# An MLP gate row built in four column tiles and spread over the partitions by DMA, and a ScalarE normalisation cut into single instructions

## The chip, the core and the metric

One of the eight cores of a Trainium2 chip runs the whole program. The metric is device time in microseconds (us) for one execution, as the median of several executions; lower is better. The engines are named as the profile names them: PE (TensorE, matrix products), PEld (its weight loads), DVE (VectorE), ACT (ScalarE), POOL (GpSimd) and SP (SyncE, which here only starts transfers). Transfers started by SP run in hardware queue q1, those started by POOL in software queue q0; sixteen DMA engines serve both.

## The reference, cut to what matters

Sequence length S = 2048, model width D = 576, hidden width 4608, bf16 data.

```python
mod = (silu(c) @ w_mod).reshape(1, 6, 1, 576)
sa, ca, ga, sb, cb, gb = (mod[:, k] for k in range(6))
h = layernorm(x) * (1 + ca) + sa
x = x + ga * A(h)          # dilated local attention: 32 heads of 18, 8 keys, every second row
h = layernorm(x) * (1 + cb) + sb
x = x + gb * (((h @ w_gate) * (h @ w_up)) @ w_down)
```

The change concerns gb, the gate row of the MLP: 576 numbers, the same for every row of the sequence, each a dot product of silu(c) with a column of the last sixth of w_mod. It also concerns how one layernorm is written out.

## The kernel before, in words

The 2048 rows are cut into 8 chunks of 256 rows. The chunks are handled in five groups, [0], [1, 2], [3, 4], [5, 6], [7]. For each group the MLP has a gate-up phase (`gate_up`) and a down phase (`down`, `down_last` for the last). In gate-up, step f (0 to 35) makes 128 of the 4608 hidden columns: two products g and u over 576 = 4 x 128 + 64 inputs. They are done as a `Pair`: the array is used as two halves of 64 rows, one for g and one for u; `first()` does the 64-row rest and four half blocks, `second()` swaps the halves. The order on PE is first of step f, then second of step f-1. ACT then copies u and g out of PSUM (lines 757 and 758 for one-chunk groups), and DVE multiplies them (line 760) once per two steps. Weight blocks of four steps (`wgu`, gate half and up half, 512 KB each) come by SP in queue q1; the down weights (`wd`, 576 KB a block) come by POOL in queue q0. PSUM is one pool of 8 banks which are given out in turn (line 91), so a product needs the bank that was given out eight tiles before to have been read.

Into the steps are woven the attention pieces of later chunks. Their order is not found at run time: the function `timed` (lines 808 to 845) walks through the 36 steps with a clock t for PE and one for DVE, and puts a piece behind the first step at which its condition holds. A piece is (PE time, DVE time, marks it needs, its own mark, delay until that mark holds, function). The products of the next chunk (`qkv_of`, nine `Pair`s: four pairs of q and k column tiles, tile 4 on its own, and two for v) are put between steps in the same way, at most one per step. Every engine then executes its instructions in the order in which they were written. SP and POOL too: a transfer that waits for something holds up the transfers behind it on the same engine.

All the changed pieces lie in the gate-up phase of group 0 (some 48 to 98 us in the profile). Named from the trace and the planner:

- Line 1271, the first thread of group 0: `load_wm5` (lines 1015 to 1017: the last sixth of w_mod, 512 rows into the spare part of `hh`, 64 rows into `wm5r`, which the trace calls o_t), `load_wd(0)`, `both_halves`, and, when 12.0 on the planner's clock have passed, `gb_row` at a planned PE time of 1.5.
- `gb_row` (line 1257) calls `mod_row` (lines 349 to 359) and then `ld_d1(3)`, the load of down block 3. `mod_row` has silu(c) on all 128 weight columns (`sc_bc`), so each of its ten products (five with 512 columns into pa, five with 64 into pb) writes the same row on all 128 partitions; two ACT copies bring it to `gb_bc` (f32). `gb_row` stands behind step 11, that is, directly ahead of step 12, which is the first to need weight block 3.
- Weight block 3 lies in the spare part of `hh` too and is loaded at line 1320; block 4 is asked for at step 4, block 5 at step 8, block 6 at step 12.
- `norm_of(3, ...)` (line 683): layernorm of chunk 3: statistics (`a_ln(3)`), `rsq`, two ACT pieces e3 and n3 (one per 128 rows j; each of them `norm_act`, line 283: a small DVE product `ln_nb`, an ACT instruction of 576 columns and one of 64 columns, which doubles the last 64 columns), then `a_td(3)`: two DMA transposes by SP (line 394) into hT, and `a_mod(3)`: five DVE instructions on hT (line 302, planned 8.0 behind the transposes), which set mark h3. The nine pairs of chunk 3 need h3.
- Line 1273: layernorm of chunk 4: `a_ln(4)` on DVE, `rsq`, and two ACT pieces (`norm_act` with 576 columns only, no doubling); in the trace ACT line 287 at 79.00 and 82.65.
- `values_of(1)`: DVE products and sums of the attention of chunk 1 (lines 514, 521 to 524).
- `gb_bc` is read by DVE behind the down products (lines 949, 954 and 996).

Of the kernel before, what the change touches and what calls it, by code (L numbers as in the profile page):

```python
# [7 lines left out]
BF = mybir.dt.bfloat16  # L8
F32 = mybir.dt.float32
ALU = mybir.AluOpType  # L10
# [8 lines left out]
P = 128  # L19
D = 576  # L20
DP = 640
KT = 5
KF = 4
H = 32
# [2 lines left out]
DIL = 2  # L27
FF = 4608
FT = FF // P
HALO = 16  # L30
SPAN = 14
EPS = 1e-5
# [2 lines left out]
ST = CH // P  # L35
# [9 lines left out]
def kernel(  # L45
# [13 lines left out]
    nc = tc.nc  # L59
# [9 lines left out]
    consts = pool("consts", 1)  # L69
    wts = pool("wts", 1)  # L70
    dramp = pool("dramp", 1, space=DRAM)
    xin = pool("xin", 2)
    xres = pool("xres", 2)
    small = pool("small", 2)
# [16 lines left out]
    def ps(shape, dt, name):  # L91
        return psp.tile(shape, dt, name=name, tag="bank")
# [8 lines left out]
    eps = consts.tile([P, 1], F32, name="eps")  # L101
    modc = consts.tile([P, 4, KT], F32, name="modc")
    ga_bc = consts.tile([P, D], F32, name="ga_bc")
    gb_bc = consts.tile([P, D], F32, name="gb_bc")
    sc_bc = consts.tile([P, KT, P], BF, name="sc_bc")
    xns = [consts.tile([P, ST, DP], BF, name=f"xn{k}") for k in range(2)]
    o_sb = consts.tile([P, ST, DP], BF, name="o_sb")
# [5 lines left out]
    wv = wts.tile([P, KT, D], BF, name="wv")  # L113
    wo = wts.tile([P, KT, D], BF, name="wo")
    vd = dramp.tile([HALO + S, D], BF, name="vd")
    prod_t = consts.tile([P, 4 * KT * CH], BF, name="prod_t")
    prod_n = [0]

# [19 lines left out]
    def load_res(i):  # L138
        x_res[i] = xres.tile([P, ST, D], BF, name="x_r")
        nc.sync.dma_start(x_res[i][:], x_rows(i))  # L140

    wgu_blk, wgu_in, wd_blk, wd_home, wgu_home = {}, {}, {}, {}, {}
    NG = len(GROUPS)
    NBLK = FT // FB

# [17 lines left out]
    def load_wd(g):  # L163
        if g >= NG * NBLK:
            return
        r0 = (g % NBLK) * FB * P
        wb = wd_home.pop(g, None)
        if wb is None:
            wb = wdp.tile([P, FB, D], BF, name="wd")
        wd_blk[g] = wb  # L170
        return nc.gpsimd.dma_start(wb[:], B_w_down[r0:r0 + FB * P, :].rearrange("(k p) n -> p k n", p=P))  # L171
# [88 lines left out]
    def ln_parts(src, tag, act=False, both=None):  # L260
        stats = small.tile([P, ST, 2, 6], F32, name="ln_stats" + tag)
        mv = small.tile([P, ST, 2], F32, name="ln_mv" + tag)
        rstd = small.tile([P, ST], F32, name="ln_rstd" + tag)
        xn = xns[turn[0] % 2]
        turn[0] += 1
        both = tag == "b" if both is None else both

        def stat(j, hfs=(0, 1)):
            for hf in hfs:
                nc.vector.bn_stats(stats[:, j, hf, :], src(j)[:, hf * 288:(hf + 1) * 288])  # L270
            if hfs[-1] == 1:
                nc.vector.bn_aggr(mv[:, j, :], stats[:, j, :, :].rearrange("p a b -> p (a b)"))

        def rsq(r):
            nc.scalar.activation(rstd[:, r], mv[:, r, 1], ACTF.Ln, bias=eps[:])
            nc.scalar.activation(rstd[:, r], rstd[:, r], ACTF.Exp, scale=-0.5)

        def norm(j):
            for d0, s0, n in ((0, 0, D), (D, D - 64, 64))[0:2 if both else 1]:
                nc.vector.tensor_scalar(xn[:, j, d0:d0 + n], src(j)[:, s0:s0 + n], mv[:, j, 0:1], rstd[:, j:j + 1],  # L280
                                        ALU.subtract, ALU.mult)

        def norm_act(j):
            nb = small.tile([P, 1], F32, name="ln_nb")
            nc.vector.scalar_tensor_tensor(nb[:], mv[:, j, 0:1], -1.0, rstd[:, j:j + 1], ALU.mult, ALU.mult)
            for d0, s0, n in ((0, 0, D), (D, D - 64, 64))[0:2 if both else 1]:
                nc.scalar.activation(xn[:, j, d0:d0 + n], src(j)[:, s0:s0 + n], ACTF.Identity, bias=nb[:], scale=rstd[:, j:j + 1])
        return xn, stat, rsq, (norm, norm_act) if act is None else norm if not act else norm_act

    def layernorm(src, tag, act=False, both=None):  # L290
        xn, stat, rsq, norm = ln_parts(src, tag, act, both)
        for j in range(ST):
            stat(j)

        def norms(js=range(ST)):
            for j in js:
                norm(j)
        return xn, lambda: rsq(slice(0, ST)), norms

    def modulate(dst, s, m, vi_scale, vi_shift, on_dve):  # L300
# [20 lines left out]
    def mod_columns(wm, pi, fill=lambda: None, steps={}):  # L321
        pm = ps([P, 320], F32, "pm")
        order = (KF, 0, 1, 2, 3)
        for kt in order:
            for q in range(4):
                rows = slice(0, P) if kt < KF else slice(64 * (q // 2), 64 * (q // 2) + 64)
                c0 = (q // 2) * D + (q % 2) * 256
                nc.tensor.matmul(pm[H * q:H * (q + 1), :], lhsT=sc_bc[rows, kt, 0:H], rhs=wm[rows, kt, c0:c0 + 320],
                                 start=(kt == order[0]), stop=(kt == order[-1]), skip_group_check=True)
            steps.get(kt, nop)()  # L330
        mrow = sp.tile([P, 320], BF, name="mrow")
        nc.scalar.copy(mrow[:], pm[:])
        fill()
        tr = ps([P, 3, P], BF, "pm_t")
        for n in range(2):
            nc.tensor.transpose(tr[:, n, :], mrow[:, n * P:(n + 1) * P], ident[:])
        for r in (slice(0, 64), slice(64, P)):
            nc.tensor.transpose(tr[r, 2, :], mrow[:, 2 * P:], ident[:])
        c01 = slice(2 * pi, 2 * pi + 2)

        def adds():
            nc.vector.tensor_tensor(modc[:, c01, 0:KF].rearrange("p b (u v) -> p b u v", v=2),
                                    tr[:, 0:2, :].rearrange("p v (b u x) -> p b u v x", b=2, u=2)[:, :, :, :, 0],
                                    addc[:, :, 0:KF].rearrange("p b (u v) -> p b u v", v=2), ALU.add)
            nc.vector.tensor_tensor(modc[:, c01, KF:KT], tr[:, 2, :].rearrange("p (b x) -> p b x", b=2)[:, :, H:H + 1],
                                    addc[:, :, KF:KT], ALU.add)
        return adds

    def mod_row(wm, dst):
        pa = ps([P, 512], F32, "pa")  # L350
        pb = ps([P, 64], F32, "pb")
        for p_t, c0, c1 in ((pa, 0, 512), (pb, 512, D)):
            for kt in range(KT):
                m = wm(kt)
                rows = slice(0, m.shape[0])
                nc.tensor.matmul(p_t[:], lhsT=sc_bc[rows, kt, :], rhs=m[:, c0:c1],
                                 start=(kt == 0), stop=(kt == KT - 1))
        nc.scalar.copy(dst[:, 0:512], pa[:])
        nc.scalar.copy(dst[:, 512:D], pb[:])
# [3 lines left out]
    aa, bb, h2T, x1 = {}, {}, {}, {}  # L363
# [319 lines left out]
    def norm_of(n, after, free, load=None):  # L683
        def go():
            a_td(n)
            if load is not None:
                load_x(load)
        act = n == 3
        norm = [(0, 0, f"r{n}", f"e{n}", 2.0, lambda: aa[n]["norm"]((0,))), (0, 0, f"e{n}", f"n{n}", 1.6, lambda: aa[n]["norm"]((1,)))]
        if not act:  # L690
            norm = [(0, 1.5, f"r{n}", f"n{n}", 0.3, lambda: aa[n]["norm"]())]
        return [(0, 2.5 if act else 2.3, after, f"m{n}", 0.2, lambda: a_ln(n)), (0, 0, f"m{n}", f"r{n}", 1.0, lambda: aa[n]["rsq"]()),
                *norm, (0, 0, f"n{n} {free}", f"x{n}", 8.0, go),
                (0, 1.6, f"x{n}", f"h{n}", 1.2, lambda: a_mod(n, (4, 0, 1, 2, 3)))]
# [166 lines left out]
    def gate_items(gi):  # L861
        n = len(GROUPS[gi])
        own = 0.15 * n + 0.06
        if gi != 1:
            return [("f", f, 1.0 * n, own, "") for f in range(FT)]
        return [("f0", f, 1.04, 0.28, "") for f in range(HEAD)] + [("f1", f, 1.04, 0.28, "h2") for f in range(HEAD)] + [("f", f, 2.0, own, "") for f in range(HEAD, FT)]

# [43 lines left out]
    def down(gi, hh, bg):  # L911
        grp = GROUPS[gi]
        nj = ST * len(grp)
        last = FT - FB
        at, late = among(last, 0.25 * nj, bg)
# [94 lines left out]
    wm5r = outp.tile([P, D], BF, name="o_t")  # L1010

    def wm5():
        return spare[0][:, 8 * NB:8 * NB + FB * D].rearrange("p (k d) -> p k d", d=D)

    def load_wm5():
        nc.gpsimd.dma_start(wm5(), w_mod[0:KF * P, 5 * D:6 * D].rearrange("(k p) n -> p k n", p=P))
        nc.gpsimd.dma_start(wm5r[0:64, :], w_mod[KF * P:D, 5 * D:6 * D])

# [236 lines left out]
        load_wd(k)  # L1255

    def gb_row():
        mod_row(lambda k: wm5()[:, k, :] if k < KF else wm5r[0:64, :], gb_bc)
        ld_d1(3)

    first = attention_of(1, 2)[12:-14]
# [6 lines left out]
    at = [k for k, p in enumerate(first) if p[3] == "o11"][0] + 2  # L1268
    first[at] = (0.6, 0, "o11", "-", 0, lambda: b_o(1))
    gbg = {0: (qkv_of(3, "p17 z3"),  # L1270
               [[(0, 0, "", "-", 0, lambda: (load_wm5(), load_wd(0))), (0, 0, "", "z3", 8.0, both_halves), (0, 0, "", "w5", 12.0, nop), (1.5, 0, "w5", "-", 0, gb_row), (0, 0, "", "-", 0, lambda: load_res(2))],
                first,
                norm_of(3, "", "", 5) + [(0, 2.5, "", "m4", 0.2, lambda: a_ln(4)), (0, 0, "m4", "r4", 1.0, lambda: aa[4]["rsq"]()),
                                         (0, 0, "r4", "e4", 2.0, lambda: aa[4]["norm"]((0,))), (0, 0, "e4", "n4", 1.6, lambda: aa[4]["norm"]((1,))),
# [37 lines left out]
    for gi, grp in enumerate(GROUPS):  # L1312
        hh_t = hhp.tile([P, FT * 2 * CH], BF, name="hh")
        n = CH * len(grp)
# [45 lines left out]
```

## Time and profile before

| | |
|---|---|
| median of 3 runs | 543.81 us (543.6, 543.81, 544.0) |
| the profiled execution, its own time | 544.44 us |
| its span, first to last instruction | 542.7 us |
| granted PE clock | 1.000 |
| gate row: its ACT copies (lines 358, 359) | 0.585 + 0.218 us |
| ACT line 287, 576 columns; 64 columns | 0.87 us; 0.42 us |
| POOL memset of 64 x 576 bf16 (lines 230, 231, 249) | 0.57 to 0.59 us |
| POOL transfer of 72 KB (line 1017), issue | 0.56 us |
| up half of weight block 3 (SP, issued 41.67), to landing | 22.9 us |
| landing of: w_mod rows, wm5r, wd block 0, wd block 3 | 60.7, 61.0, 63.2, 65.3 us |

The span is shorter than the profiled execution's own time by 1.7 us, which lies outside its instructions. Times inside the trace are counted from the start of the span. Busy shares say little here: a PE matrix product is counted from its start to its end although the next one starts 0.1 us later, so PE is shown busy in many places where it loses up to 0.2 us.

### The profile page before, as it was taken

To read this page: it belongs to the slowest core of one execution; us is meant where nothing else is said; L and a number is where in the kernel's file an instruction comes from. 1 tells how busy PE (TensorE), PEld (TensorE's weight loads), DVE (VectorE), ACT (ScalarE), POOL (GpSimd) and SP (SyncE) were. 2 spreads that over 40 slices of the span, in tenths; PEclk is the share of its full clock that TensorE was granted. 3 is DMA by queue.
4 is the path that set the end of the run, shared out by engine and by line. 5 is a ranking of instruction groups with operands and counts; after the bars stand their busy time and mean duration, and the time that the engine had idled before them with its cause. 6 is when DMAs were issued, how large, how long until landed. Compare 5 with 4: busy or idle time off the path is not lost.

```text
span 542.7 us, 14569 instructions
## 1 busy us (share of the span) xinstructions
PE 535.3 (99%) x6157; PEld 321.9 (59%) x6189; DVE 315.9 (58%) x713; ACT 251.5 (46%) x617; POOL 67.9 (13%) x104
## 2 busy tenths in 40 slices
PE   8999999999999999999999999999999999999997
PEld 4887789756745444555544444555544445558875
DVE  4989586777766777646358896524344924032212
ACT  4776777543566553022645552014555551006630
POOL 7104012122000110111000110110010101010210
PEclk9999999999999999999999999999999999999999
DMA  8999999778872694878435983894296592849821
GB/s 264 299 261 363 336 272 332 258 224 258 267 203 89 211 208 153 227 220 293 135 108 163 232 288 68 162 239 159 89 275 176 156 311 69 255 138 294 271 74 42
DMA packets 94924, 114.52 MB, mean 211 GB/s; under 512 B 27980, under 2 KB 83676, under 8 KB 94732
## 3 DMA queue, kind: packets, MB, share of 16 engines
q1 hardware_dynamic: 83360, 67.29, 44.6%
q0 software_dynamic: 11344, 46.25, 27.8%
q8 instruction: 48, 0.79, 0.6%
q14 instruction: 16, 0.13, 0.1%
q10 hardware_dynamic: 156, 0.07, 0.0%
HBM read 103.15 MB, written 4.74 MB: 199 GB/s over the span
## 4 chain that ended last, share of the span: by engine, by line
PE 94%; DMA 3%; DVE 1%; SPq 1%; ACT 1%; issue 0%
PE pg L706 28%; PE pu L706 23%; PE acc L921 19%; PE pq L706 3%; PE accr L926 3%; PE pw L605 3%; PE pq L416 3%; PE acc L976 3%; PE lgT L470 2%; DMA wmC<-in_w_mod_dram 2%; PE pv L706 2%; PE pv L439 1%; DMA wqk<-in_A_wqkv_dram 1%; PE po L567 1%; PE pwj L584 0%
## 5 line engine op out<-in xcount | busy, mean ns | idle before, releaser
L706 PE MATMUL pg<-h2T,wgu 64*128 64x512 bf16 (+1 forms) x1376 | 265.5, 331 | 0.0
L706 PE MATMUL pu<-h2T,wgu 64*128 64x512 bf16 (+1 forms) x1376 | 264.5, 331 | 0.0
L706 PEld LDWEIGHTS <-wgu 64*128 64x128 bf16 x2752 | 136.5, 94 | 94.8 <-issue 0.5
L757 ACT CAST u_sb<-pu 128x512 bf16<-128x512 f32 (+1 forms) x172 | 85.4, 497 | 135.8 <-PE pg L706 131.2
L760 DVE TENSOR_TENSOR hh<-g_sb,u_sb 128x512 bf16<-128x512 bf16 x136 | 57.4, 423 | 116.2 <-ACT g_sb L758 115.7
L758 ACT CAST g_sb<-pg 128x512 bf16<-128x512 f32 (+1 forms) x172 | 86.7, 504 | 0.0
L921 PEld LDWEIGHTS <-hh 128*128 128x128 bf16 x504 | 49.0, 98 | 59.5 <-issue 1.5
L921 PE MATMUL acc<-wd,hh 128*128 128x512 bf16 x329 | 84.1, 380 | 0.1
L926 PE MATMUL accr<-wd,hh 128*128 128x64 bf16 x344 | 62.4, 193 | 0.7
L706 PE MATMUL pu<-h2T,wgr 64*128 64x512 bf16 (+1 forms) x188 | 61.5, 327 | 0.2 <-ACT u_sb L757 0.2
L706 PE MATMUL pg<-h2T,wgr 64*128 64x512 bf16 (+1 forms) x188 | 61.5, 327 | 0.0
L926 PEld LDWEIGHTS <-hh 128*128 128x128 bf16 x504 | 45.8, 98 | 1.9
L171 POOL DMA_DIRECT2D wd<-in_B_w_down_dram x29 | 21.8, 752 | 190.0 <-PE accr L926 93.4
L461 DVE TENSOR_TENSOR prod_t<-qT,kT 128x1280 bf16<-128x1280 bf16 x56 | 43.7, 818 | 0.7 <-ACT kT L777 0.7
L514 DVE TENSOR_TENSOR vsh<-vsh,attn 128x1152 bf16<-128x1152 bf16 x56 | 39.6, 748 | 1.2 <-DMA vsh<-vd 1.2
L706 PEld LDWEIGHTS <-wgr 64*128 64x128 bf16 x376 | 19.7, 94 | 15.4 <-issue 2.5
L921 PE MATMUL acc<-prod_t,hh 128*128 128x512 bf16 x111 | 28.8, 380 | 0.0
L304 ACT ACTIVATE h2T<-h2T,modc 128x256 bf16<-128x256 bf16 x12 | 6.6, 595 | 45.3 <-DMA h2T<-xn 45.3
L455 POOL DMA_DIRECT2D vsh<-vd x14 | 12.5, 897 | 104.8 <-DVE o_sb L524 89.6
L706 PE MATMUL pq<-hT,wqk 64*128 64x256 bf16 (+1 forms) x360 | 22.2, 259 | 0.1
L416 PE MATMUL pq<-hT,wqk 128*128 128x256 bf16 (+1 forms) x225 | 21.2, 251 | 0.4 <-ACT hT L304 0.4
L926 PE MATMUL accr<-prod_t,hh 128*128 128x64 bf16 x112 | 21.6, 193 | 0.1
(208 smaller groups left out, 605.0 us busy)
## 6 DMA issues: line engine op xcount, KB each, us to landing
wgu<-in_B_w_gate_dram SPq DMA_DIRECT2D x41, 512.0 KB, 4.5
wgu<-in_B_w_up_dram SPq DMA_DIRECT2D x41, 512.0 KB, 6.4
wd<-in_B_w_down_dram POOLq DMA_DIRECT2D x29, 576.0 KB, 5.6
vsh<-vd POOLq DMA_DIRECT2D x14, 1152.0 KB, 9.3
prod_t<-in_B_w_down_dram POOLq DMA_DIRECT2D x8, 576.0 KB, 7.6
hh<-in_B_w_down_dram POOLq DMA_DIRECT2D x6, 576.0 KB, 6.4
x_r<-in_A_x_dram SPq DMA_DIRECT2D x8, 288.0 KB, 8.3
vd<-v_sb POOLq DMA_DIRECT2D x16, 144.0 KB, 5.2
```

Source lines behind the costliest of these rows:

```text
L171: return nc.gpsimd.dma_start(wb[:], B_w_down[r0:r0 + FB * P, :].rearrange("(k p) n -> p k n", p=P))
L416: nc.tensor.matmul(pq[:, gi, :], lhsT=wqk[:, kt, m * P:(m + 1) * P], rhs=hT[:, kt, cols], start=(kt == order[0] and not (by_k and gi)), st ...
L461: nc.vector.tensor_tensor(prod, aa[i]["qT"][:], aa[i]["kT"][:, :, off:off + CH], ALU.mult)
L514: nc.vector.tensor_tensor(v, v, at, ALU.mult)
L605: nc.tensor.matmul(pw[:], lhsT=oT[:, m, js(j)], rhs=wo[:, m, 0:512], start=(m == 0), stop=(m == KT - 1))
L706: return nc.tensor.matmul(out, lhsT=lhs, rhs=rhs, start=first, stop=last, skip_group_check=True)
L757: nc.scalar.copy(u[:, c, :], pu)
L758: nc.scalar.copy(g[:, c, :], pg)
L760: return lambda: nc.vector.tensor_tensor(hh[:, f - c:f + 1, :], g, u, ALU.mult)
L921: nc.tensor.matmul(acc[j][:], lhsT=hh[:, f, js(j)], rhs=wb[:, f % FB, 0:512], start=(f == 0), stop=(f == FT - 1))
L926: nc.tensor.matmul(accr[:, j, :], lhsT=hh[:, f, js(j)], rhs=wb[:, f % FB, 512:D], start=(f == 0 and j == 0), stop=(f == FT - 1), skip_grou ...
L976: nc.tensor.matmul(acc[i][:], lhsT=hh[:, f, js(j)], rhs=wb(f)[:, c0:c1], start=(f == 0), stop=(f == FT - 1))
```

## The change

Gate row. `mod_row` for gb is replaced by a new function. The matrix products use 32 columns of weights instead of 128, and four of them stand side by side in the array: column tile q makes columns 144 q to 144 q + 143 of the row on partitions 32 q to 32 q + 31. That is 20 products of 144 columns in place of 10, and one PSUM bank in place of two. One ACT copy brings the 128 x 144 result to `grow` (bf16). POOL writes one partition of each tile to DRAM (`gd`, 4 x 144) and then reads `gd` back with a partition step of zero into `gb_bc`, which is now bf16 and has the row on all partitions. `grow` has 576 columns, of which 144 are used, so that it and `gb_bc` together take as many bytes as `gb_bc` in f32 did. As the 64-row rest is now multiplied as a full 128-row block, POOL clears the other 64 partitions of `wm5r` first. `ld_d1(3)` is still behind the row, so on POOL it now follows the two new transfers. The planned PE time of the piece is 0.85 instead of 1.5.

```diff
-    gb_bc = consts.tile([P, D], F32, name="gb_bc")
+    gb_bc = consts.tile([P, D], BF, name="gb_bc")
+    grow = consts.tile([P, GR], BF, name="grow")
...
+    gd = dramp.tile([4, GC], BF, name="gd")
...
+    def gb_cols(wm):
+        pa = ps([P, GC], F32, "pa")
+        for kt in range(KT):
+            for q in range(4):
+                nc.tensor.matmul(pa[H * q:H * (q + 1), :], lhsT=sc_bc[:, kt, 0:H], rhs=wm(kt)[:, GC * q:GC * (q + 1)],
+                                 start=(kt == 0), stop=(kt == KT - 1), skip_group_check=True)
+        nc.scalar.copy(grow[:, 0:GC], pa[:])
+        nc.gpsimd.dma_start(gd[:], grow[0:P:H, 0:GC])
+        nc.gpsimd.dma_start(gb_bc[:], bass.AP(gd.tensor, gd.offset, [[0, P], [1, D]]))
...
     def load_wm5():
+        nc.gpsimd.memset(wm5r[64:, :], 0.0)
...
     def gb_row():
-        mod_row(lambda k: wm5()[:, k, :] if k < KF else wm5r[0:64, :], gb_bc)
+        gb_cols(lambda k: wm5()[:, k, :] if k < KF else wm5r[:])
         ld_d1(3)
...
-               [[..., (0, 0, "", "w5", 12.0, nop), (1.5, 0, "w5", "-", 0, gb_row), ...],
+               [[..., (0, 0, "", "w5", 12.0, nop), (0.85, 0, "w5", "-", 0, gb_row), ...],
```

Normalisation. `norm_act` takes the parts it is to do (0: the 576 columns, 1: the 64 doubled ones) and makes `ln_nb` only once per j. In `norm_of` the two ACT pieces of chunk 3 become four, one per instruction: e30, e31, e32 with a delay of 1.0 each and n3 with 1.6, where there were e3 with 2.0 and n3 with 1.6.

```diff
-        norm = [(0, 0, f"r{n}", f"e{n}", 2.0, lambda: aa[n]["norm"]((0,))), (0, 0, f"e{n}", f"n{n}", 1.6, lambda: aa[n]["norm"]((1,)))]
+        norm = [(0, 0, f"r{n}" if k == 0 else f"e{n}{k - 1}", f"e{n}{k}" if k < 3 else f"n{n}", 1.0 if k < 3 else 1.6, lambda k=k: aa[n]["norm"]((k // 2,), (k % 2,)))
+                for k in range(4)]
```

More of the change, by code (lines that the diff above doesn't have):

```diff
@@ L29 @@
 FT = FF // P
+GC = D // 4
+GR = D
 HALO = 16
@@ L281, in norm, with norm_act @@
                                         ALU.subtract, ALU.mult)
[L283 to L286, printed above, removed]
+        nbs = {}
+        def norm_act(j, parts=(0, 1)):
+            if j not in nbs:
+                nbs[j] = small.tile([P, 1], F32, name="ln_nb")
+                nc.vector.scalar_tensor_tensor(nbs[j][:], mv[:, j, 0:1], -1.0, rstd[:, j:j + 1], ALU.mult, ALU.mult)
+            nb = nbs[j]
+            for d0, s0, n in [((0, 0, D), (D, D - 64, 64))[p] for p in parts if p == 0 or both]:
                 nc.scalar.activation(xn[:, j, d0:d0 + n], src(j)[:, s0:s0 + n], ACTF.Identity, bias=nb[:], scale=rstd[:, j:j + 1])
@@ L293, in layernorm, with norms @@
             stat(j)
-        def norms(js=range(ST)):
+        def norms(js=range(ST), *parts):
             for j in js:
-                norm(j)
+                norm(j, *parts)
         return xn, lambda: rsq(slice(0, ST)), norms
@@ L1270 @@
     gbg = {0: (qkv_of(3, "p17 z3"),
-               [[(0, 0, "", "-", 0, lambda: (load_wm5(), load_wd(0))), (0, 0, "", "z3", 8.0, both_halves), (0, 0, "", "w5", 12.0, nop), (1.5, 0, "w5", "-", 0, gb_row), (0, 0, "", "-", 0, lambda: load_res(2))],
+               [[(0, 0, "", "-", 0, lambda: (load_wm5(), load_wd(0))), (0, 0, "", "z3", 8.0, both_halves), (0, 0, "", "w5", 12.0, nop), (0.85, 0, "w5", "-", 0, gb_row), (0, 0, "", "-", 0, lambda: load_res(2))],
                 first,
```

## The prediction

> **What bounds the kernel now.** The page first: busy times and the chain that ended last.
>
> ```profile
> span 542.7 us, 14569 instructions
> PE 535.3 (99%) x6157; PEld 321.9 (59%) x6189; DVE 315.9 (58%) x713; ACT 251.5 (46%) x617; POOL 67.9 (13%) x104
> PE 94%; DMA 3%; DVE 1%; SPq 1%; ACT 1%; issue 0%
> ```
>
> PE sets the end, so PE time taken out counts, unless PE then meets something that did not move with it. Hence the second view, the chain in order of time from 49 to 66 us, where the row is made (start, length, what):
>
> ```profile
> 57.40 1.20 ACT xn L287 x2
> 61.02 0.66 PE lgT L470 x20
> 62.77 0.32 PE pa L356
> 63.15 0.91 PE pa L356 x3
> 64.06 0.36 PE pb L356 x5
> ```
>
> The row costs PE 0.32 + 0.05 + 0.91 + 0.36 = 1.64 us, and the two ACT instructions of chunk 3's norm are in the chain with 1.20. Third, the timeline of the weight loads:
>
> ```profile
> 58.91 0.11 PEld L706 LDWEIGHTS <-wgu 64*128 64x128 bf16 x3 [0.46 <-issue]
> 64.63 0.33 PEld L706 LDWEIGHTS <-hh 64*128 64x128 bf16 x7 [0.28 <-DMA hh<-in_B_w_up_dram]
> 81.03 0.42 PEld L706 LDWEIGHTS <-wqk 64*128 64x128 bf16 x8 [0.33 <-issue]
> ```
>
> Three gaps: 0.46 us behind that norm (the copy of u, due about 57.7, starts at 58.51, and PE needs its bank), 0.28 right behind the row for the up half of weight block 3, and 0.33 at 81.03, when ACT has just freed banks of chunk 3's pairs. Fourth, the DMA share of the two queues, from 60 to 61 us and (last line) from 65 to 66 (packets, MB, engine share):
>
> ```profile
> q1 hardware_dynamic: 61, 0.06, 20.7%
> q0 software_dynamic: 62, 0.26, 78.5%
> ```
>
> ```profile
> q1 hardware_dynamic: 352, 0.35, 108.6%
> ```
>
> While POOL's q0 has data, q1 gets a packet for a packet, but of 1 KB against over 4 KB: 0.06 MB per us. Alone it gets 0.35. Fifth, DVE and ACT from 72 to 80 us:
>
> ```profile
> 72.33 1.37 DVE L302 TENSOR_SCALAR hT<-hT,modc 128x256 bf16<-128x256 bf16 x5 [1.40 <-DMA hT<-xn]
> 76.81 2.08 DVE L514 TENSOR_TENSOR vsh<-vsh,attn 128x1152 bf16<-128x1152 bf16 x3
> 78.81 0.15 DVE L285 SCALAR_TENSOR_TENSOR ln_nb<-ln_mva,ln_rstda 128x1 f32<-128x1 f32 x1
> 79.00 0.87 ACT L287 ACTIVATE xn<-x_t,ln_nb,ln_rstda 128x576 bf16<-128x576 bf16 x1 [0.19 <-DVE ln_nb L285]
> ```
>
> From the landing of chunk 3's transposes (call it T; 72.33) DVE works without a pause, and 6.48 us later makes the ln_nb that chunk 4's norm on ACT waits for. That chain will decide.
>
> **The row.** 20 products replace 10. No row has 144 columns in column tiles. Nearest above: lgT, the same 20 in four column tiles, 256 columns each, 0.66. Nearest below: 20 products of 32 columns on the whole array (lgj L1076 in the chain), 0.49; four side by side with 144 take the column time of 36. I take 0.50, nearest to the 32-column row, and keep 0.49 to 0.66. Between weight loads, lgT adds to the 0.98 of a plain step 52.11 - 50.27 - 0.98 = 0.86, its 0.66 and the switches around it; so the new row adds 0.86 - 0.16 = 0.70. The old one adds 64.22 - 61.61 - 0.98 = 1.63. Taken out: **0.9** (0.77 to 0.94).
>
> A rule speaks against it: the Trainium skill ("TensorEngine Tiling (Array Packing)", Restrictions and Gotchas) says that column tiling excludes fast weight load. If the 20 loads (96 ns each, L470) came one behind the other, the row would take 1.9 us and lose 0.3 where I gain 0.9. The trace does not bear that out: lgT's 32-column loads take 92 to 97 ns, as the 98 of full loads, and its 20 pairs 0.66 in all.
>
> One ACT copy of 144 columns replaces 0.585 + 0.218: nearest rows 128x128, 0.27, and 128x256, 0.37; ACT saves about 0.5 in a stretch where it isn't in the way. POOL's clearing of wm5r (0.57 to 0.59 by L249 and its like) starts when its last transfer is issued, 50.33, and ends at 50.9, where the w_mod load started at 50.77: 0.2 late. Hidden: that queue was behind until w_mod landed at 60.7, and the row starts at 62.7. Without that cover it would cost its 0.2. The bf16 gate row on DVE: L954 takes 690 ns with the f32 row; no row has a bf16 second operand beside PSUM; the all-bf16 sum of 576 (L524, 0.46) bounds the gain at 0.28 for each of the last three products, 0.6 in all at the end; below, nothing. I take nothing, since the f32 PSUM operand stays.
>
> **The norm.** The copy of u waits for 0.87 instead of 1.20, so the gap of 0.46 loses **0.34** (0 to 0.46). The 64-column instructions come one step later, 0.36 each pipelined; ACT has 0.45 free per step (0.98 less 0.53 for two copies), and PE has four pairs of banks. Covered; uncovered, 0.36 each. The transposes stay behind step 10, and SP isn't free for them before 64.98 anyway.
>
> **The POOL queue.** Behind the row stand now the write of gd (waits for ACT's copy, about 63.8), the read of gd (waits until the write has landed) and then wd block 3, which in the trace was issued at 52.86, ran in q0 from about 61.4 to 64.1 and landed at 65.3. So q0 runs dry at 61.4, and q1 has 0.35 per us instead of 0.06 to 0.22. The up half of block 3 lands about 1.5 earlier (2.1 us of q0 at some 75% of the engines), at 63.1 instead of 64.57. PE arrives 0.9 + 0.34 earlier, at 63.1: the 0.28 is gone too, and step 12 is **1.5** ahead. Block 4 (68.1, now 66.6; needed 66.9) follows. Block 3 of wd is not used before the down phase at 98; behind it on POOL stand blocks 1, 4 and 2, which were issued at 79.17 and later (they wait for weight block 6) and find POOL free by 72.
>
> When does the displaced data come? Write of gd issued about 63.9, landing: the 144 KB writes of v into DRAM at 18.38, 21.24 and 40.38 took 6.0 with q1 full, the 18 KB one at 2.25 took 2.2 with nothing beside it (the line is that of 40.38):
>
> ```profile
> vd<-v_sb POOLq DMA_DIRECT2D x1, 144.0 KB, 6.0
> ```
>
> q1 is full until 69, so I take 6 (bounds 2.2 and 6.0): landed 69.9, the read issued 70, block 3 at 70.7. By then the transposes are through: in q1 they follow block 5, and everything there is 1.5 ahead: T = **70.8** instead of 72.33 (70.3 to 71.6). gd's read and block 3 (0.74 MB, 2.5 us of q0) then fall on weight block 6, which landed about 78.9 and is needed at 80: 1.5 earlier plus at most 2.0 is 79.4. Just covered.
>
> **The planner.** With 0.85 for 1.5 its clock is 0.65 lower behind step 11, so a_mod(3) moves from behind step 17 to 18 and the pairs from behind steps 19 to 25 to 20 to 26; from step 28 all is where it was. PE's work is the same, but its place against DVE isn't. Chunk 4's first norm stays behind step 21, with the same DVE work ahead of it from T on. Before, three pairs (up to tile 4) had been started when ACT came to it; now two have.
>
> New times: ln_nb at T + 6.48, ACT starts at T + 6.67 and ends at T + 7.54; the copies of pair (2,3) behind it free its banks at T + 8.2, and only then can PE start pair (5,6), which comes eight tiles later. PE would be there at 77.9 and waits until T + 8.26 = 79.06. Before, at 81.03, PE had the same work done and pair (5,6) besides (0.98). So the kernel stands 79.06 + 0.98 - 81.03 = **-0.99** against before, in general T - 71.8: of the 1.5 us and the 0.33 gap, about 0.8 goes into the new wait. ACT then has two pairs to catch up, chunk 4's second norm at T + 10.4; I find PE short by 0.1 at the first v pair, nothing later. Sum: -0.9 on this execution (span 542.7, its own time 544.44, 0.6 over the median); against the median 543.81 - 0.95 = **542.85**.
>
> **Rivals.**
> *The displaced load hits the transposes* (slower). If the write of gd lands as fast as the 18 KB one, at 66, q0 fills from about 66.6 to 69.5, while block 5 and the transposes run; q1 keeps a fifth, so they lose 2.0: T = 72.8, and by T - 71.8 the kernel is 1.0 slower, 544.8. It decides from T = 71.8 on, a landing before about 68. For it: the write is 1.2 KB. Against: the 6.0 us rows. By the Trainium skill ("DMA: Bandwidth & Descriptors", Anatomy of one DMA) a POOL transfer takes 2.0 us and a size term, so gd lands at 65.9 and this is the case; the trace agrees only where q1 is empty.
> *The DVE chain does not bind*: DVE or ACT makes up what I count as waiting, or T falls to 70. All of 1.5 + 0.33 stays: 542.0. For it: PE's four pairs of banks; against: ACT did wait 0.19 for ln_nb before, with PE later.
> *It does not do what it says*: block 3's up half isn't freed by q0, or the row costs 0.66 and the new steps collide; the saved PE time is spent waiting at step 12 and T stays 72.3: 0 to +0.5, 543.8 to 544.3.
>
> **Chances.** Forecast 0.47 (own range 542.3 to 543.6, from T), late transposes 0.30, no binding chain 0.12, nothing done 0.11. A measurement tells about 0.2%, 1.09 us. Faster: 0.21 of the forecast's, all 0.12 of no chain, 0.02 = 0.35. Slower: 0.18 of the late transposes' (T can pass 72.9 when block 5 is late too), 0.05 of nothing done = 0.23. The same: 0.42. Range 541.9 (no chain, with a little of the DVE tail) to 545.0 (T at 73).
>
> **What would show it.** The row at 0.5 in the chain; the gap at 58.9 near 0.1; the 0.28 gone; no q0 data between 62 and 70; a_mod's first DVE instruction near 70.8; ACT idle 2 us before chunk 4's first norm and PE short of banks for 1 us ahead of pair (5,6). Wrong if a_mod starts after 72, or if that wait isn't there.

## The result, and the profile after

The changed kernel takes 545.17 us (median of 22 runs, 543.12 to 547.26) where the kernel before took 544.01 beside it (22 runs, 543.47 to 545.67): a ratio of 1.002 with an interval of 1.0010 to 1.0029. On two more occasions it came to 544.32 (ratio 1.0008, 0.9993 to 1.0022) and 544.80 (1.0003, 0.9990 to 1.0015). The ratio and its interval take in every execution, so they can part from the quotient of the medians. The changed kernel is the same or up to 0.3% slower; the forecast of 542.85 is missed, and 545.17 lies 0.17 above its range.

The profiled execution took 544.71 us. Its page (the span; the shares of the chain that ended last; the group of products for u with the idle time ahead of it) looks much like that of before, but for the last item:

```profile
span 543.0 us, 14593 instructions
...
PE 91%; DMA 4%; DVE 2%; ACT 1%; SPq 1%; issue 0%; DVEq 0%
...
L725 PE MATMUL pu<-h2T,wgu 64*128 64x512 bf16 (+1 forms) x1376 | 264.7, 331 | 1.1 <-DMA wgu<-in_B_w_up_dram 1.1
```

PE waits 1.1 us for an up half of the weights; before, that group waited for none. The timeline of the weight loads (start, length, engine, line, operation, in brackets the idle time before and what ended it) says where:

```profile
58.69 0.85 PEld L725 LDWEIGHTS <-wgu 64*128 64x128 bf16 x16
61.62 0.10 PEld L725 LDWEIGHTS <-wgr 64*128 64x128 bf16 x2 [0.44 <-DVE dd L513]
62.71 0.31 PEld L361 LDWEIGHTS <-sc_bc 128*32 128x32 bf16 x20 [0.21 <-issue]
63.15 0.43 PEld L725 LDWEIGHTS <-hh 64*128 64x128 bf16 x8
...
78.67 0.09 PEld L725 LDWEIGHTS <-wqk 64*128 64x128 bf16 x1 [0.46 <-issue]
78.94 0.42 PEld L725 LDWEIGHTS <-wqk 64*128 64x128 bf16 x8 [0.18 <-issue]
...
93.25 0.77 PEld L725 LDWEIGHTS <-wgu 64*128 64x128 bf16 x15 [1.41 <-DMA wgu<-in_B_w_up_dram]
...
100.88 1.19 PEld L434 LDWEIGHTS <-wqk 128*128 128x128 bf16 x10
```

The reader is to see four things. The row is short (20 loads in 0.31 us) and the step behind it starts at 63.15 without the 0.28 us wait for block 3. The bank wait that was forecast is there, 0.46 + 0.18 us ahead of pair (5,6). At step 32 the first of 16 loads runs at 91.74, and then PE stands until 93.25 for the up half of weight block 8. And the last line, a query product behind step 35, is a milestone. In the kernel before, the row's first loads, the loads of step 32 (without a wait) and the milestone stood at

```profile
62.70 0.55 PEld L356 LDWEIGHTS <-sc_bc 128*128 128x128 bf16 x4 [0.21 <-issue]
...
92.84 0.86 PEld L706 LDWEIGHTS <-wgu 64*128 64x128 bf16 x16
...
100.60 1.19 PEld L416 LDWEIGHTS <-wqk 128*128 128x128 bf16 x10
```

From the milestone to the end of the span it is 542.7 - 100.6 = 442.1 us before and 543.0 - 100.88 = 442.1 after, and 442.1 to 442.2 in every trace of this study. So the kernels don't differ behind 101 us. Ahead of it, the row's first load stands at 62.70 and 62.71. It stood between 62.25 and 64.10 in the traces, by execution more than by kernel, since the parts changed here lie behind 57 us. What a kernel is worth is therefore read from one number, the **stretch** from the row's first load to the milestone: 37.90 us before and 38.17 after, +0.27, as the spans (542.7 and 543.0) say. It is read from one execution of each kernel, and it too varies: three traces of the changed kernel gave 37.83 to 38.52, two of one kernel below (h1 and i2) 37.72 and 36.69. Differences of some tenths in it show little; the wait at step 32 is the firmer sign.

In POOL's list of transfers and DVE's timeline, the chain of the row and the landing T:

```profile
64.39 0.61 POOL L364 DMA_DIRECT2D gd<-grow  x1 [11.30 <-ACT grow L363]
70.22 0.57 POOL L365 DMA_DIRECT2D gb_bc<-gd  x1 [5.22 <-DMA gd<-grow]
70.79 0.78 POOL L175 DMA_DIRECT2D hh<-in_B_w_down_dram  x1
79.59 0.76 POOL L175 DMA_DIRECT2D wd<-in_B_w_down_dram  x1 [8.01 <-DMA wgu<-in_B_w_up_dram]
```

```profile
70.75 1.45 DVE L310 TENSOR_SCALAR hT<-hT,modc 128x256 bf16<-128x256 bf16 x5 [0.44 <-DMA hT<-xn]
77.30 0.15 DVE L292 SCALAR_TENSOR_TENSOR ln_nb<-ln_mva,ln_rstda 128x1 f32<-128x1 f32 x1
```

Down block 3 is issued at 70.79 and T is 70.75, as forecast. The fourth line is the first of down blocks 1, 4 and 2 (1.77 MB), which wait for weight block 6. The up half of weight block 8, issued at 80.55 (82.62 before), took 12.7 us to land (8.6 before), after and then before:

```profile
wgu<-in_B_w_up_dram SPq DMA_DIRECT2D x1, 512.0 KB, 12.7
```

```profile
wgu<-in_B_w_up_dram SPq DMA_DIRECT2D x1, 512.0 KB, 8.6
```

The DMA share of the queues from 88 to 89 us, after and then before (packets, MB, share of the engines), shows what ran beside it:

```profile
q0 software_dynamic: 72, 0.28, 78.4%
q1 hardware_dynamic: 73, 0.07, 23.9%
```

```profile
q1 hardware_dynamic: 326, 0.33, 99.6%
```

Before, the three down blocks had q0 from 81 to 86 and block 8 then had the engines to itself; after, they still ran beside it.

### The profile page after: what moved, and what is told of

It is laid out like the page before. It is cut to its first block, busy times and chain, and to the rows that moved or that the text cites. A ratio compares the mean times of both kernels' runs of the same rounds, so it can differ in the third digit from the quotient of the medians.

```text
span 543.0 us, 14593 instructions
## 1 busy us (share of the span) xinstructions
PE 534.0 (98%) x6168; PEld 321.1 (59%) x6199; DVE 317.0 (58%) x713; ACT 251.1 (46%) x616; POOL 69.9 (13%) x107
## 4 chain that ended last, share of the span: by engine, by line
PE 91%; DMA 4%; DVE 2%; ACT 1%; SPq 1%; issue 0%; DVEq 0%
PE pg L725 27%; PE pu L725 21%; PE acc L940 19%; PE pq L434 4%; PE accr L945 3%; PE pw L623 3%; PE pq L725 3%; PE acc L995 3%; DMA wgu<-in_B_w_up_dram 2%; PE pv L457 2%; PE lgT L488 1%; PE pv L725 1%; DMA wmA<-in_w_mod_dram 1%; DMA hT<-xn 1%; PE po L585 1%; DVE vsh L532 0%
```

## The experiments

The wait at step 32 and the stretch are those of the one profiled execution of each kernel. Kernels of one letter ran on one chip beside the kernel before; one kernel differed by up to 0.3% between occasions, so medians are compared within a letter, and the stretch, with the care said above, across letters.

| kernel | median, us | ratio to before (interval) | wait at step 32 | stretch |
|---|---|---|---|---|
| before, after (first) | 544.01, 545.17 | 1.0020 (1.0010 to 1.0029) | 0, 1.41 | 37.90, 38.17 |
| e1 old planned time | 545.02 | 1.0023 (1.0009 to 1.0037) | 1.50 | 37.70 |
| e2 down block 3 late | 543.28 | 0.9987 (0.9976 to 0.9999) | 0 | 36.76 |
| e3 the same in before | 544.04 | 0.9996 (0.9987 to 1.0005) | 0 | 37.21 |
| e4 down block 3 first | 545.14 | 1.0017 (1.0004 to 1.0029) | 0 | 37.13 |
| f1 norm split alone | 544.11 | 0.9998 (0.9985 to 1.0012) | 0 | 37.21 |
| f2 row alone | 544.26 | 0.9999 (0.9986 to 1.0011) | 1.90 | 38.16 |
| f4 as e4 | 543.92 | 0.9986 (0.9971 to 1.0000) | 0 | 37.41 |
| f5 down block 3 at step 22 | 544.69 | 1.0003 (0.9987 to 1.0019) | 0.31 + 1.39 | 38.53 |
| g1 after, again | 544.32 | 1.0008 (0.9993 to 1.0022) | 0.21 + 1.40 | 37.83 |
| g2 as e2 | 543.37 | 0.9987 (0.9973 to 1.0002) | 0 | 36.72 |
| g3 e2 with the old row | 543.50 | 0.9988 (0.9980 to 0.9997) | 0 | 37.21 |
| g4 down block 3 twice | 543.98 | 1.0007 (0.9989 to 1.0024) | 0 | 36.42 |
| h1 down blocks 1, 4, 2 behind block 7 | 542.95 | 0.9972 (0.9961 to 0.9983) | 0 | 37.72 |
| h2 h1 and e2 | 542.93 | 0.9972 (0.9962 to 0.9982) | 0 | 36.64 |
| h3 after, a third time | 544.80 | 1.0003 (0.9990 to 1.0015) | 1.62 | 38.52 |
| h4 as e2 | 543.04 | 0.9969 (0.9955 to 0.9983) | 0 | 36.18 |
| i1 h1 with the old row | 544.10 | 1.0000 (0.9987 to 1.0014) | 0 | 37.45 |
| i2 as h1 | 543.48 | 0.9989 (0.9973 to 1.0005) | 0 | 36.69 |

### The planner, and the place of down block 3 (e1 to e4)

e1: the changed kernel planned as the old one.

```diff
-... (0.85, 0, "w5", "-", 0, gb_row), ...
+... (1.5, 0, "w5", "-", 0, gb_row), ...
```

> The changed kernel with the row's planned time put back from 0.85 to 1.5, so that the pairs of chunk 3 and the second logit transposes stand where they stood before. If the displaced data in q0 (read of gd, wd block 3, 0.74 MB between 74 and 78.5 us) is what makes weight block 8 late, its up half still lands after 92.5 and PE still waits for it at step 32, 0.5 us or more: time 544 to 545.5. If the order of the plan is the cause (logit transposes queued behind block 7, so that they meet the three wd loads at 81 us), the wait goes and the kernel is 0.5 to 1.5 us faster than before: 542.5 to 543.5.

The wait at step 32 stayed (1.50 us), and so did the time. The order of the pieces isn't the cause.

e2: down block 3 asked behind step 35. e3: the same edit in the kernel before.

```diff
     def gb_row():
         gb_cols(lambda k: wm5()[:, k, :] if k < KF else wm5r[:])
-        ld_d1(3)
...
-    loads = {(0, 20): ...
+    loads = {(0, 35): lambda: ld_d1(3), (0, 20): ...
```

> The changed kernel with the load of wd block 3 taken from behind the row to behind step 35, after the value loads of chunk 2. Displaced data: 0.59 MB fewer ahead of weight blocks 6, 7 and 8, so block 8's up half lands at least 1.5 us earlier than 93.25, the wait at step 32 (1.41) goes, and the 1.1 us that PE was ahead there stay: 542.5 to 543.3. Order of the plan: the transposes still meet the wd loads at 81, block 8 lands after 92.5, and the time is 544 to 545.5.

> The kernel before with only the load of wd block 3 moved behind step 35. If q0's wd block 3 is what held up the up half of weight block 3, that lands near 63.1 instead of 64.57, the 0.28 us gap behind the row goes, the transposes of chunk 3 land near 70.8, and the 0.33 gap at 81 goes with them: 0.3 to 0.7 us faster, 543.2 to 543.6. If the row alone brought that, the up half still lands at 64.5 and the time is that of before.

e2 has no wait at step 32 and is the first kernel that is faster than before, by 0.13%. In e3 the 0.28 us wait for block 3 is gone and the stretch is 0.69 us shorter, but its median moved by only 0.1, against 0.3 to 0.7 expected. Nor does the trace show that down block 3 had held up weight block 3: f1 below leaves down block 3 where it was, and has no such wait either and the same stretch of 37.21.

e4 (and f4, the same kernel on another occasion): down block 3 asked ahead of the row, so that it doesn't stand behind gd.

```diff
     def gb_row():
+        ld_d1(3)
         gb_cols(lambda k: wm5()[:, k, :] if k < KF else wm5r[:])
-        ld_d1(3)
```

> The changed kernel with the load of wd block 3 ahead of the row on POOL, so that it is issued near 53 as before; the row, its two transfers and the norm stay as changed. Displaced data: the up half of weight block 3 lands near 64.5 again, PE waits about 1.4 us for it at step 12, the transposes land near 72.3, and by (landing - 71.8) the kernel is 0.5 us slower than before at the pairs of chunk 3; in return block 8 is there in time. 543.8 to 544.6, with a spread like that of the kernel before. Order of the plan: block 8 is late here too, by as much as in the changed kernel or more: 545 or over.

> The kernel with wd block 3 ahead of the row on POOL once more, for a second trace. In the first trace weight block 3 had landed at 57, four to six us earlier than in the others, with a time at the low end of that kernel's runs (543.51 of 543.5 to 547.0). If wd block 3 ahead of the row costs by holding up weight block 3, a trace near the median shows PE waiting 0.5 to 1.5 us at step 12 and T at 72 or later; if the loss is elsewhere, PE waits at step 32 as in the changed kernel.

The wait at step 32 is gone in both traces, the bank wait at 78.9 is larger (0.80 and 1.06), and the times contradict each other: 1.0017 and 0.9986. What it is worth stays open.

### The two halves of the change, and a fourth block at step 22 (f1, f2, f5)

f1 is the kernel before with the split norm alone, f2 the changed kernel with the norm's two old pieces.

> The kernel before with only the norm of chunk 3 cut into four steps. The gap of 0.46 us behind the norm falls to about 0.13, but PE then comes to weight block 3 that much earlier and waits for it, so nothing is left: within 0.3 us of the kernel before. If the four steps are what slows the changed kernel (an ACT instruction in the wrong place), this one is slower by 0.5 us or more.

> The changed kernel with the norm of chunk 3 put back to two steps; the row, its transfers and wd block 3 behind them stay. If weight block 8's landing sets the end, the norm doesn't matter: PE comes to step 32 about 0.3 us later, waits 0.3 us less, and the time is that of the changed kernel, 544.8 to 545.6. If the norm's steps cause the loss, the time is under 543.6.

The wait at step 32 comes with the row and the transfers behind it:

```profile
94.56 0.77 PEld L724 LDWEIGHTS <-wgu 64*128 64x128 bf16 x15 [1.90 <-DMA wgu<-in_B_w_up_dram]
```

f2's median, 544.26, lies under the 544.8 to 545.6 that were expected with that wait. The norm alone changes nothing that can be measured. f5: down block 3 asked with the other down blocks.

```diff
         gb_cols(lambda k: wm5()[:, k, :] if k < KF else wm5r[:])
-        ld_d1(3)
...
-... (0, 22): lambda: load_wd(2), ...
+... (0, 22): lambda: (load_wd(2), ld_d1(3)), ...
```

> The changed kernel with the load of wd block 3 taken from behind the row to behind step 22, as the fourth of the down blocks that POOL issues from 79 us on. If all that counts is how much q0 moves ahead of weight block 8 (which is asked for at step 24, just behind), 0.59 MB are still ahead of it: its up half lands at 93 or later, PE waits 1 us or more at step 32, 544.8 to 546. If it is the place of the load, 74 to 78 us, among blocks 6 and 7 and the transposes, that does the harm, block 8 lands near 91.4 and the time is 542.8 to 543.6.

Only gd's read is displaced onto block 6 here (down block 1 is issued at 78.42, 1.2 us earlier than after), and yet block 8 is late, by 0.31 us in its gate half and 1.39 in its up half. So it isn't the delay of block 6 alone that counts; 2.36 MB of down blocks now stand in q0 ahead of block 8.

### The bytes, or their order (g1 to g4)

g1 is the changed kernel, g2 is e2, g3 is f1 with e2's edit; g4 loads down block 3 twice.

```diff
         ld_d1(3)
+        ld_d1(3)
```

> The changed kernel, unaltered, beside the next three on one chip: calls differ by up to 0.3% for one kernel (the kernel with block 3 first gave 1.0017 and 0.9986), so only this call compares these four. Theory (the down block 3 and the read of gd, moved to 70 to 75, push the weight blocks back until the up half of block 8 is late for step 32): a wait of 1.2 to 1.9 us for in_B_w_up_dram in the weight loads near 92 to 94, 544.6 to 545.6 us. Rival (the first trace was an accident of one execution's DMA): no such wait, within 0.1% of before.

> The changed kernel with down block 3 asked behind step 35. Theory: no wait at step 32, 1.0 to 1.5 us below the changed kernel of this call, 0.5 to 1.0 us below before. Rival (the gain seen once was the chip's): equal to the changed kernel within 0.1%.

> The kernel before with the norm split and with down block 3 asked behind step 35: all of the late-block kernel but the four-tile row. The rest of what its time is above that kernel's is the row's own worth. Theory: 543.9 to 544.2, so the row alone is worth 0.7 to 0.9 us where nothing is pushed back. Rival (the late block itself brings the gain): as fast as the late-block kernel with the row, 543.3.

> The changed kernel with down block 3 loaded twice in a row at its place: 0.59 MB more through the same queue at 71 to 76 us. Theory: the wait at step 32 grows from 1.4 by the 1.5 to 2 us that 0.59 MB take of both queues at 0.3 to 0.4 MB per us, unless it lands after block 7 and takes an earlier step too; 546.5 to 547.5 us. Rival (step 32 is late from the order on POOL or from a shift of the whole schedule, not from the bytes): the wait and the time stay within 0.3 us of the changed kernel's.

g1 has the wait again, g2 hasn't. g3, with the old row, is within 0.13 us of g2 in the median, against the 0.7 to 0.9 expected, so by the medians its rival came nearer; the stretches differ by 0.49. g4 went against its theory: with 0.59 MB more the wait vanished from the trace, and its median is 0.34 us under g1's, though its ratio (1.0007 against 1.0008) is not lower. POOL's list in g4 says where to look:

```profile
70.86 0.78 POOL L175 DMA_DIRECT2D hh<-in_B_w_down_dram  x1
80.87 0.76 POOL L175 DMA_DIRECT2D hh<-in_B_w_down_dram  x1 [9.24 <-DMA hh<-in_B_w_down_dram]
81.62 0.75 POOL L175 DMA_DIRECT2D wd<-in_B_w_down_dram  x1
```

The second load writes where the first does and waits until that has landed; on POOL the down blocks 1, 4 and 2 stand behind it and are issued 2.0 us later (81.62, not 79.59). By the shares of the queues, q0 is in force again from 86, where after it was so from 83, and block 8, asked at 80.61, has landed 9.3 us later, at 89.9. Why q0 starts 3 us later where POOL is only 1.3 to 2.0 us later, the list doesn't say. The theory that block 8 is late by the number of all bytes had to go; its place was taken by what stands ahead of block 8, that is, by their order.

### The order alone (h1 to h4)

h1 is the changed kernel with one number changed: the same bytes, another order. h2 adds e2's edit; h3 is the changed kernel, h4 is e2.

```diff
-... (0, 20): lambda: behind(load_wd(1), wgu_in[6]), ...
+... (0, 20): lambda: behind(load_wd(1), wgu_in[7]), ...
```

> The changed kernel with one word changed: the down blocks 1, 4 and 2 wait for weight block 7 instead of weight block 6; down block 3 stays right behind the row. Theory A (their 1.77 MB in q0 get in front of the up half of weight block 8, and moving down block 3 behind the row only brought that collision about): the wait of 1.4 us at step 32 is gone though no byte less is moved; 542.8 to 543.8 us. Theory B (the bytes of down block 3 and gd between 74 and 79 are what block 8 is late by, whatever runs behind): the wait stays above 1 us, within 0.3 us of the changed kernel of this call.

> Both: down block 3 behind step 35 and the down blocks 1, 4, 2 behind weight block 7. Theory A: no wait at step 32 either way, so within 0.3 us of the late-block kernel. Rival: the loads of the next chunk or the down blocks themselves come late for step 35 or for the down phase at 98, 0.5 us or more above the late-block kernel.

> The changed kernel a third time, beside the other three on one chip. The time from the row's first weight load to the first query product behind step 35 was 38.17, 37.83 and 37.70 us in three traces with the wait at step 32 and 37.90 in the kernel before; the rest of the span is 442.1 us in each. Expected: the wait of 1.2 to 1.9 us again, 37.5 to 38.5, 544.2 to 545.2 us. Rival (the wait comes in some executions only): none, near 36.8 and 543.5.

> The changed kernel with down block 3 behind step 35, a third time. Expected: no wait at step 32, 36.7 us from the row to the query product, 543.2 to 543.7 us, 0.1 to 0.2% below before. Rival: the two earlier results were the chips', equal to before.

h1 is 1.85 us faster than the changed kernel beside it (542.95 against 544.80) and 0.28% faster than before; no run of it (highest 544.32) reaches the changed kernel's median. POOL's list in h1:

```profile
71.61 0.78 POOL L175 DMA_DIRECT2D hh<-in_B_w_down_dram  x1
82.96 0.76 POOL L175 DMA_DIRECT2D wd<-in_B_w_down_dram  x1 [10.57 <-DMA wgu<-in_B_w_up_dram]
```

and the loads of step 32, which wait for nothing:

```profile
92.65 0.10 PEld L725 LDWEIGHTS <-wgr 64*128 64x128 bf16 x2
92.67 0.86 PEld L725 LDWEIGHTS <-wgu 64*128 64x128 bf16 x16
```

Down block 3 is where the change put it and just as large, the other three are issued behind block 7 (82.96), and block 8, asked at 81.11, lands after 8.1 us, at 89.2:

```profile
wgu<-in_B_w_up_dram SPq DMA_DIRECT2D x1, 512.0 KB, 8.1
```

The profiled execution of h1 was its slowest: its stretch of 37.72 holds a stop of 0.97 us at 70.74, which no other trace has there. It isn't a wait for a bank, as i2's expectation below has it: PE stops in the middle of a step, after 11 of 16 loads, and the profile shows no cause. h2 is no faster than h1, as it must be if both cures remove the same wait. h3 shows the wait in the changed kernel a third time, h4 that e2's gain is real.

### What the order is worth without the row (i1, i2)

i1 is f1 with h1's edit, i2 is h1.

> The kernel before with the norm split and the down blocks 1, 4, 2 behind weight block 7; the row is the old one of two products, and down block 3 stands where it stood. What it is above the next kernel is what the four-tile row and the moved down block 3 are worth once the order of the loads lets them. Theory: nothing was late at step 32 here, so the order changes nothing: 37.2 us from the row to the query product, 543.8 to 544.3 us, 0.8 to 1.2 us above the next kernel. Rival: the order of the loads alone is the gain, and this is as fast as the next kernel.

> The changed kernel with the down blocks 1, 4, 2 behind weight block 7, a second time. Expected: no wait at step 32, 36.4 to 36.8 us from the row to the query product unless the bank wait of 0.97 us at 70.7 shows again (then 37.7), 542.7 to 543.3 us, 0.2 to 0.3% below before. Rival: the first result was the chip's.

The order alone brings nothing (1.0000). On top of it the row and the moved down block 3 bring 0.62 us in the median and 37.45 - 36.69 = 0.76 in the stretch, a little less than expected. In i2 block 8 landed 6.6 us after it was asked. There q1 is alone until 87 and moves 1.20 MB from 83 to 87; in the changed kernel, beside q0, it moves 0.77 MB from 83 to 90. One of i2's microseconds, 85 to 86:

```profile
q1 hardware_dynamic: 340, 0.35, 108.4%
```

i2's gain against before, 0.11%, is smaller than h1's 0.28%, and its interval includes 1. That h1 is faster than before is shown by one occasion well and by the other weakly; that it is faster than the changed kernel rests on h1 beside h3.

## Why the prediction was wrong

**What failed.** The step "gd's read and block 3 (0.74 MB, 2.5 us of q0) then fall on weight block 6 ... Just covered". Block 6 was covered: it had landed at 79.59, when POOL went on, and 79.4 was forecast, and PE didn't wait for it. But the sentence stopped there. Behind block 6, down blocks 1, 4 and 2 (1.77 MB) are tied to its landing, and they share the engines with blocks 7 and 8. While q0 has data, q1 gets about 0.07 MB per us (88 to 89 us). The forecast knew this rate, and used it for block 3, for the transposes and for block 6, but asked of no later block when it lands. Block 8 had 1.7 us in hand before: landed 82.62 + 8.6 = 91.2, needed 92.94. After, it was needed at 91.84 and landed at 93.25. The 0.74 MB that were moved in are some 2.1 us of both queues at 0.35 MB per us, and 2.0 is what it landed later; with down block 3 out of the way (e2) it landed at 91.43. But what counts is the bytes that stand ahead of block 8: with the same bytes and the down blocks behind block 7 (h1), it landed at 89.2. The two cures aren't equally safe. Where down block 3 is moved (e2, g2, h4, and e4 and f4), block 8 lands at 91.1 to 91.9, 0.2 us or less ahead of its need; in h1, h2 and i2 it has 3.5 us or more in hand.

**The balance of the stretch**, from the timelines: row and its switches -1.12 (first load of the row to the next step's: 1.56 before, 0.44 after), wait for block 3 -0.28, old bank wait at 81.03 -0.33, new bank waits +0.64, block 8 +1.41: +0.32, measured +0.27. The two waits that went (0.28 and 0.33) stood in one execution of the kernel before; f1 has neither.

**The steps that held.** Block 3's up half landed at 42.44 + 20.2 = 62.6 (63.1 forecast) and the 0.28 is gone. That the emptied q0 brought this isn't shown, and may be luck: with down block 3 in its old place the up half landed anywhere from 57.3 (e4) to 64.6 (before), with it moved from 57.8 (g3) to 63.5 (e3). gd's write, issued 64.39, had landed when its read was issued at 70.22, 5.8 us later (6 taken). The number held, but the rows that it came from are no good ground for it: the 144 KB of 40.38 were through q0 in the first us (0.15 MB from 40 to 41), while gd's packets show in q0 only from 68 to 70, and the 18 KB row wasn't alone, as the prediction says (q1 moved 0.25 MB from 2 to 3 us and 0.13 from 3 to 4). T came at 70.75 (70.8), ln_nb at 77.30 (77.28), and the wait for banks is at its place. Up to step 32 the kernel stood 1.1 us ahead of before (0.99 forecast), with sizes that were off in both directions.

**Sizes that were off.** The row was worth 1.09 us of PE, not 0.9: it adds 63.14 - 61.62 - 0.98 = 0.54 to a step, where 0.70 was taken from the switches around lgT; its 20 products show as 0.43 in the chain (0.50 taken):

```profile
62.78 0.43 PE pa L361 x20
```

The new bank wait is 0.64 us, not the 1.16 that 77.9 to 79.06 made, and ACT stood 0.94 us for ln_nb, not 2. The norm split took 0.33 off the gap at 58.9, as forecast (0.34), but 0.23 of it came back two steps on: PE waits 0.44 for DVE's dd at 61.62, where it waited 0.21. DVE's chain through mx and dd hadn't been followed. The norm's worth is 0.1, and f1 measures none.

**The rule against column tiles.** The price that the prediction set on it, 20 loads one behind the other in 1.9 us, wasn't paid: they took 0.31. The Trainium skill ("TensorEngine Tiling (Array Packing)", Restrictions and Gotchas) says that column tiling excludes fast weight load; that section gives no time for it, and no run here shows which kind of load these were.

**The rivals.** Late transposes didn't happen: gd landed at 69.9. In fifteen traces POOL waited between 4.5 and 6.0 us for that write, so the slow write was the right choice. The Trainium skill ("DMA: Bandwidth & Descriptors", Anatomy of one DMA) gives such a transfer 2.0 us and a size term; none of the fifteen agrees. None of the rivals was the one that came, a late weight block two places on, and its place in the chances was missing.

**The rest of the miss.** By stretch, 36.9 was forecast (37.90 - 0.99) and 38.17 came: 1.3 of the 2.3 us. The other 1.0 lies in the executions: before's profiled run was 0.63 above the median that the forecast went from, and after's 0.46 below its own. With the changed kernel at 544.3 and 544.8 on the other occasions, its place inside or outside the range is a matter of a few tenths; that it isn't faster is not.

**What stays open.** How much of the row's 1.1 us is kept once block 8 is in time: 0.13 (g2 against g3) to 0.62 us (i2 against i1) by medians, 0.49 to 0.76 by stretch, differences that are no larger than those between traces of one kernel. Part of the rest goes into waits for PSUM banks near 78: h4, whose trace has none, has a stretch of 36.18, 1.03 under g3's. And why e4 was slow once and fast once: with 0.2 us in hand at step 32 in both of its traces, other executions may have waited there, but none was traced.

## What to carry to other kernels

When a transfer is moved, follow it not only to the block that it lands on but to every transfer that is tied to that block, up to the first one with a deadline; a saving on PE pulls the deadlines in (1.1 us here) while the move pushes the landings out (2.0 us here). Where a low-priority stream (needed at 98) can start ahead of an urgent one (needed at 92), tie it to a later event: one number in one line was worth 1.85 us in the changed kernel, more than the row, and nothing in the kernel that had nothing late. When doubling a suspect removes the symptom, look at what the doubled piece delays.

## What the runs showed of the hardware

A small write can take nearly as long as a large one: gd's 1.1 KB landed 5.5 us after its issue, the 144 KB of 40.38 after 6.0, both with q1 busy beside them. Both queues nearly stop at times: from 82 to 83 us in the changed kernel,

```profile
q0 software_dynamic: 5, 0.02, 21.3%
q1 hardware_dynamic: 74, 0.04, 13.7%
```

while the second of lg_t's DMA transposes was under way (issued 74.44, 9.5 us to landing), and as at 74 in the kernel before, where it was issued at 73.67 (0.02 MB in that us). That the transposes cause the hole was not tried. And executions of one kernel differ ahead of the row (its first load at 62.25 to 64.10 us in three traces of the changed kernel) and in the stretch (36.69 and 37.72 in h1's kernel), while the 442.1 to 442.2 us behind the milestone repeated in all twenty traces.
